# Fourteen expert-weight loads cut into 28 halves, one in each attention slot from 2 to 29

## The chip, the core and the metric

The kernel runs on one core of a Trainium2 chip. The metric is the device time of one execution in microseconds (us), the median of several runs. One more execution was taken with the hardware profiler; all rows below are from that one.

The engines of the core, as the profile names them: PE does matrix products and transposes through the array (PEld is its weight load), DVE and ACT do elementwise work, POOL does small copies and here also issues one kind of DMA, and SP only issues DMAs. DMAs issued by POOL run as queue q0 (software descriptors), those issued by SP as queue q1; both share 16 DMA engines.

## The reference: what is computed

Block-causal attention over 8 batches, 8 heads, 576 positions and 64 columns a head, followed by a mixture of experts on the 512 columns of the heads together. In short:

```python
scores = (q @ k.T) / sqrt(64)            # masked by blocks of 64
x = softmax(scores) @ v                  # (8, 576, 512)
logits = x @ w_gate                      # 8 experts
e = argmax(logits), or the expert of the position before where
    sigmoid(x @ w_local) >= 0.5          # a chain along each batch
out = p[e] * (relu(x @ w1[e]) @ w2[e])   # w1: 512x1024, w2: 1024x512
```

There are 4608 rows and 8 experts; each row goes through one expert alone.

## The kernel before: slots of attention, then tiles of rows

**Attention** runs as 32 slots, `i = 0 .. 31`, one for each pair of heads of a batch. A slot does the products with `v` of the pair before (`values`, line 998), its own scores (line 977) and exponentials, and the transposes of `k` and `q` of the pair after (`transposes(i + 1)`, tile `kq`, line 692). Its inputs come in stages: SP issues the loads of `k` and `q` of pair `i + 2` at the slot's start (`load_qk`, lines 867 and 872) and of `v` of pair `i + 1` (line 889); near the slot's end POOL copies `k` and `q` of pair `i + 2` into the order that the transposes want (`arrange`, line 880). PE reads the arranged copy in the slot after.

**Beside attention** two more things go through POOL's instruction stream. The finished rows `x` and their factors are stored to a table in DRAM (`x_rows`, line 677): the stores are held back during a slot and issued by POOL at its end (`release`). And the experts' weights are loaded with a cast from f32 to bf16: `load_weights(e, layer)` issues one DMA for all of `w1[e]` (line 107, 128 partitions x 4 rows of 1024) or of `w2[e]` (line 111, 128 x 8 rows of 512), 1 MB each as it lands. Fourteen of them, experts 0 to 6, go out in the even slots 2 to 28:

```python
if wload < 2 * E - 2 and i == 2 + 2 * wload:
    load_weights(*divmod(wload, 2))
    wload += 1
```

The last expert's two loads are placed apart, since its space is scratch and staging until then: `w1[7]` among the first gathers in slot 29 (the list `pending`), `w2[7]` at the end of slot 30. The staging of even pairs lies in the space of `w2[6]`.

**The experts** follow. The rows, sorted by expert, are gathered in tiles of 128 (`gather`, line 651, POOL), transposed by a DMA that SP issues (line 1269 for the first four tiles, 1393 after), multiplied by `w1` (`first_mm`, line 1093) and by `w2` (`second_mm`, line 1335). Which expert a tile belongs to is known only at run time, so the slice of `w2_bf` that `second_mm` reads is dynamic, and its first product waits for the loads of all eight `w2`. PE does the work in a fixed order: `first_mm` of tile 0, `first_mm` of tile 1, `second_mm` of tile 0, and so on.

What sets the order: every engine's stream is fixed when the kernel is built, in the order in which the Python code emits it. A POOL DMA carries one of eight completion semaphores in rotation (`order` of a POOL stream shows them as waits), so each waits for the one eight before it. The last part of the routing (the chain of lines 313 to 397 and `slots_first`, lines 430 to 537) is interleaved with the slots on DVE and PE.

Of the kernel before, what the change touches and what calls it, by code (L numbers as in the profile page):

```python
# [62 lines left out]
def kernel(  # L63
# [11 lines left out]
    nc = tc.nc  # L75
# [10 lines left out]
    Dm = H * D  # L86
    E = moe_w_gate.shape[1]
    F = moe_w1.shape[2]
    BS = B * S
    P = 128  # L90
# [11 lines left out]
    w1_bf = w_p.tile([P, E * KO1 * F], BF16, tag="w1", name="w1_bf")  # L102
    w2_bf = w_p.tile([P, E * FO * Dm], BF16, tag="w2", name="w2_bf")
    WE = KO1 * F
    def load_weights(e, layer):
        if layer == 0:
            nc.gpsimd.dma_start(
                out=w1_bf[:, e * WE:(e + 1) * WE].rearrange("p (do f) -> p do f", f=F),
                in_=moe_w1[e].rearrange("(do di) f -> di do f", di=P))
        else:  # L110
            nc.gpsimd.dma_start(
                out=w2_bf[:, e * WE:(e + 1) * WE].rearrange("p (fo d) -> p fo d", d=Dm),
                in_=moe_w2[e].rearrange("(fo fi) d -> fi fo d", fi=P))

    HP = H // 2
    NPAIR = B * HP
# [715 lines left out]
    with tc.tile_pool(name="atn_const", bufs=1) as cst, \  # L832
# [24 lines left out]
        def load_qk(i):  # L857
            if i >= NPAIR:
                return
            b, p = divmod(i, HP)  # L860
            h2 = slice(2 * p, 2 * p + 2)
            tl = ld.tile([P, 2, D], F32, tag="qkl", name="qkl")
            raws[i] = [tl]
            for j, src in enumerate((k, q)):

                m = staged_of(i)[:, j].rearrange("p (h j d) -> p h j d", h=2, j=4)
                nc.sync.dma_start(
                    out=m.rearrange("p h j d -> p h (j d)"),
                    in_=src[b, h2, :512].rearrange("h (p j) d -> p h (j d)", j=4))
                raws[i].append(m)  # L870
            for j, src in enumerate((k, q)):
                nc.sync.dma_start(out=tl[64 * j:64 * j + 64],
                                  in_=src[b, h2, 512:].rearrange("h s d -> s h d"))
# [34 lines left out]
        half = []  # L908
# [19 lines left out]
        def transposes(i, ahead=0, between=lambda: None):  # L928
            if i >= NPAIR:
                return between()  # L930
            ps = psp.tile([P, 2, 512], F32, tag="sc", name="kq")


            for j in range(9):
                if j == ahead:
                    turn_tail(i)()
                    between()
                if j < 8:
                    turn_part(i, j // 4, ps, (j % 4,))
            to = qkTs[i % 2][:, :, :512]  # L940
            if i == 1:
                for copy, part in zip(copies, range(2)):
                    copy(to[:, part].rearrange("p (r s) -> p r s", r=2),
                         ps[:, :, QA * part:QA * part + QA])
            else:
                nc.scalar.copy(to.rearrange("p a (r s) -> p r a s", r=2),
                               ps.rearrange("p r (a s) -> p r a s", a=2))
# [34 lines left out]
        def exps(i, u, ps):  # L982
            if i >= NPAIR:
                return
            for col, n, c, q0 in EXPS[u]:
                rows = slice(0, P)
                nc.scalar.activation(exps_at(i, c, q0, n, rows), ps[rows, :, col:col + n],  # L987
                                     func=AF.Exp, scale=scale_attn)
# [88 lines left out]
        def weights_at(w, ev):  # L1077
            nc.vector.tensor_copy(w, w1_bf[:, bass.ds(ev, WE)])
            return w
# [21 lines left out]
        def expert(ph, j, engines=(mybir.EngineType.PE, mybir.EngineType.DVE)):  # L1101
            return nc.values_load(
                et_i[ph][0:1, j:j + 1], engines=engines, min_val=0,
                max_val=(E - 1) * WE,
                skip_runtime_bounds_check_because="the table is clamped to the last expert")

        def bf(x, n):
            return x.rearrange("p a s -> p (a s)").bitcast(BF16)[:, :n]
# [33 lines left out]
        wload = 0  # L1142
# [28 lines left out]
        def behind(i):  # L1171

            def between():
                if i % HP == 2 and i < NPAIR - 2 or i == NPAIR - HP or not routing(i) and i > 1:
                    vector(AHEAD_OF[i % HP])
                run(sums)
                if sums:
                    routing(i)

            sums = sums_of(i)  # L1180
            if sums:
                values(i - 1, between)
            else:
                values(i - 1)
                between()
            if not swap:
                add_chunks(i - 1)
            if i == NPAIR - 2:
                mask(i - 1, nc.vector)
            load_v(i + 1)  # L1190
            if i > 1 and not rows_first(i):
                vector(AFTER[i % HP])

        def rows_first(i):
            return i % HP == 3 and NPAIR // 2 < i < NPAIR - 1

        holding[0] = True
        for i in range(NPAIR):
            slot[0] = i
            load_qk(i + 2)  # L1200


            swap = i == 1
            if not swap:
                behind(i)
            if i == NPAIR - 1:

                tiles = [(0, j) for j in range(NS[0])] + [(1, j) for j in range(NS[1])]
                ev = {j: expert(*tiles[j]) for j in range(2)}
                w = weights_at(bf(Pc[0], WE), ev[0])  # L1210
            for u in range(len(UNITS)):
                ps = scores(i, u)
                if u < 2 or i < 2:
                    exps(i, u, ps)
                if u == 0:
                    if i == 0:
                        transposes(1, 8)
                        constants()
                        for h in range(2):
                            hs = slice(64 * h, 64 * h + 64)  # L1220
                            nc.sync.dma_start(
                                out=wg2[hs, :, 16 * h:16 * h + E],
                                in_=moe_w_gate.rearrange("(p h d) e -> h d p e", h=2, d=D)[h])
                            nc.sync.dma_start(
                                out=wg2[hs, :, 16 * h + E:16 * h + E + 1],
                                in_=moe_w_local.rearrange("(p h d) e -> h d p e", h=2, d=D)[h])
            if swap:
                behind(i)
            last = lambda: exps(i, 2, ps) if i > 1 else None
            if i == NPAIR - 2:  # L1230
                last()
                last = lambda: None
                run([lambda: half_batch(B - 1, 0)])
            if i:
                transposes(i + 1, 6 if swap else 0,
                           last)
            if swap:
                add_chunks(i - 1)
            if i == NPAIR - 1:
                routing(i)  # L1240
            run(turns_of(i))
            if rows_first(i):
                vector(AFTER[i % HP])
            slot[0] = i + 0.5
            if i % HP == 0 or NPAIR - 3 <= i < NPAIR - 1:
                routing(i)
            if i < NPAIR - 1:
                vector(END[i % HP])
            early_mask = i % 2 == 0 and i <= NPAIR // 2
            if early_mask:  # L1250
                mask(i - 1, nc.gpsimd)
            arrange(i + 2, [nc.gpsimd.tensor_copy] * 2)
            if not early_mask and i != NPAIR - 2:
                mask(i - 1, nc.gpsimd)
            while pending:
                pending.pop(0)()

            if wload < 2 * E - 2 and i == 2 + 2 * wload:
                load_weights(*divmod(wload, 2))
                wload += 1  # L1260
            if i < NPAIR - 1:
                release(queue=nc.gpsimd)
            if i == NPAIR - 2:

                free = bf(Sb[(NPAIR - 3) % NSB], 2 * S * 2)[:, -AHEAD * Dm:]
                xTs = {}
                for j in range(AHEAD):
                    xTs[j] = free[:, j * Dm:(j + 1) * Dm].rearrange("p (k n) -> p k n", k=KO1)
                    nc.sync.dma_start(out=xTs[j], in_=row_of_x(xgs[j]), transpose=True)
                load_weights(E - 1, 1)  # L1270
# [20 lines left out]
    with ExitStack() as ffn:  # L1291
# [143 lines left out]
        for i, (ph, j) in enumerate(tiles):  # L1435
            now, done = w, prev
            waiting = len(held)
            if i == 0:
                w = w_next
            elif i + 1 < len(tiles):  # L1440
                w = w_third if i == 1 else weights_of(i + 1)
# [28 lines left out]
            if i == behind_tile:  # L1470

                nc.gpsimd.drain()
                n = nc.values_load(used[0:1, 0:1], min_val=0, max_val=E * BS)
                with tc.If(n > NS[1] - MORE, label="more"):  # L1474
                    more_tiles()
        i = len(tiles) - 1
# [37 lines left out]
```

## Time and profile before

| | |
|---|---|
| median of 3 runs | 411.5 us (409.78 to 412.72) |
| the profiled execution | 408.54 us |
| its span, first to last instruction | 406.5 us |
| PE busy | 392.6 us (97%) |
| DVE, ACT, POOL busy | 60%, 56%, 48% |
| mean granted TensorE clock | 1.000 |
| HBM read, written | 66.88 MB, 14.70 MB |
| weight loads on q0 | 16 of 1024 KB, 9.9 us median from issue to landing |

The slots run from about 7 us to 257 us after the span's start, the experts from there to the end. An engine is busy while it works on an instruction; issuing a DMA is not counted as busy. In a list of waits a row names the engine and tile that waited, what ended the wait, and its total, count and longest.

### The profile page before, as it was taken

The page shows a single profiled execution, that of the slowest core. Times are in us where ns is not written, and L with a number is a line of the kernel's source. Part 1 is how long each engine was busy: PE and PEld are TensorE (multiplying, and loading weights), DVE is VectorE, ACT ScalarE, POOL GpSimd, SP SyncE. Part 2 cuts the span into 40 slices and gives each one's busy share as a digit, 9 for nine tenths or more (in the row PEclk, how much of TensorE's full clock was granted, in tenths as well). Part 3 has the DMA queues.
Part 4 walks back from the last instruction along what each step waited for, and adds up shares of the span by engine and source line. Part 5 has one row for each costly group of instructions (what it writes and reads, how often), then busy time and mean ns, then how long its engine had stood idle before and what let it go on. Part 6 is the DMA issues. An engine that isn't in the chain of part 4 may idle for free. (4 is left out here: it accounts for less than half of the span.)

```text
span 406.5 us, 14547 instructions
## 1 busy us (share of the span) xinstructions
PE 392.6 (97%) x5834; PEld 285.5 (70%) x5834; DVE 242.2 (60%) x505; ACT 228.7 (56%) x391; POOL 196.1 (48%) x250
## 2 busy tenths in 40 slices
PE   9999999999999999999998998998999999999985
PEld 7667677677677677667766666666777777777763
DVE  2463564564564577967899975977887333333320
ACT  3758557567557557657647465333545555555542
POOL 1244251342341342582632363074776888888833
PEclk9999999999999999999999999999999999999999
DMA  6588989999999979999989689944763645655532
GB/s 178 142 190 194 216 172 222 201 201 228 194 202 210 183 183 246 174 202 244 170 192 237 136 155 192 151 109 120 166 168 97 170 135 148 154 149 149 128 99 78
DMA packets 108819, 69.97 MB, mean 172 GB/s; under 512 B 74847, under 2 KB 100255, under 8 KB 108752
## 3 DMA queue, kind: packets, MB, share of 16 engines
q0 software_dynamic: 19200, 34.84, 41.6%
q1 hardware_dynamic: 89552, 34.19, 37.2%
q8 instruction: 48, 0.79, 0.8%
q14 instruction: 19, 0.16, 0.1%
HBM read 66.88 MB, written 14.70 MB: 201 GB/s over the span
## 5 line engine op out<-in xcount | busy, mean ns | idle before, releaser
L1019 DVE TENSOR_TENSOR S<-S,Pc 128x896 f32<-128x896 f32 (+2 forms) x96 | 84.0, 875 | 23.9 <-PE o L998 19.1
L977 PE MATMUL sc<-qkT 64*64 64x224 f32 (+6 forms) x1536 | 91.6, 367 | 0.0
L1297 DVE COPY w1c<-w_bf 128x4096 bf16 x36 | 44.3, 1231 | 55.6 <-PE ps_h L1093 52.8
L1093 PEld LDWEIGHTS <-w1c 128*128 128x128 bf16 x1152 | 67.2, 98 | 9.1 <-issue 1.3
L880 POOL COPY w_bf<-w_bf 128x512 f32<-128x512 f32 x61 | 43.9, 737 | 60.8 <-DMA w_bf<-in_k_dram 33.0
L977 PEld LDWEIGHTS sc<-qkT 64*64 64x64 f32 x1536 | 70.5, 134 | 3.7 <-issue 2.5
L1335 PE MATMUL ps_y<-w_bf,hT 128*128 x296 | 69.9, 379 | 1.0 <-DMA w_bf<-in_moe_w_dram 1.0
L987 ACT ACTIVATE Pc<-sc 128x448 f32<-128x448 f32 (+1 forms) x96 | 68.1, 716 | 0.0
L1093 PE MATMUL ps_h<-xT,w1c 128*128 128x128 bf16 x1088 | 66.3, 219 | 1.3 <-ACTq L1474 1.1
L1343 POOL DMA_INDIRECT out_dram<-y,idx x37 | 56.2, 1519 | 22.0 <-ACT y L1340 12.2
L651 POOL DMA_INDIRECT xg<-x_rows,idx x38 | 47.1, 1239 | 31.3 <-issue 13.9
L1096 ACT ACTIVATE hT<-ps_h 128x512 bf16<-128x512 f32 x76 | 45.3, 597 | 26.2 <-PE ps_h L1093 24.6
L998 PE MATMUL o<-Pc,v 128*64 128x320 f32 (+2 forms) x512 | 57.3, 366 | 0.0
L998 PEld LDWEIGHTS o<-Pc,v 128*64 128x64 f32 x512 | 34.6, 137 | 24.1
L1340 ACT ACTIVATE y<-ps_y,xg 128x512 f32<-128x512 f32 x37 | 25.4, 687 | 45.5 <-PE ps_y L1335 39.1
L987 ACT ACTIVATE S<-sc 128x576 f32<-128x576 f32 x64 | 42.0, 656 | 12.6 <-PE sc L977 12.1
L1335 PEld LDWEIGHTS <-hT 128*128 128x128 bf16 x296 | 27.5, 98 | 27.3 <-issue 1.0
L1011 ACT COPY oT<-o 128x576 f32<-128x576 f32 x32 | 20.5, 641 | 35.7 <-PE o L1007 35.7
L1026 POOL MEMSET S<- 64x128 f32 x30 | 6.0, 200 | 69.8 <-DVE S L1021 40.7
L818 DVE TENSOR_TENSOR xg<-trx,rs 128x512 bf16<-128x512 f32 (+1 forms) x31 | 20.2, 685 | 25.9 <-PE trx L692 25.8
L998 PE MATMUL o<-S,v 128*64 128x192 f32 (+1 forms) x256 | 34.7, 392 | 0.3 <-ACT qkT L925 0.3
L714 ACT COPY LT<-trg 128x320 f32<-128x320 f32 x15 | 6.4, 426 | 44.4 <-PE trg L705 44.4
(313 smaller groups left out, 467.4 us busy)
## 6 DMA issues: line engine op xcount, KB each, us to landing
w_bf<-in_moe_w_dram POOLq DMA_DIRECT2D x16, 1024.0 KB, 9.9
w_bf<-in_k_dram SPq DMA_DIRECT2D x32, 256.0 KB, 3.4
w_bf<-in_q_dram SPq DMA_DIRECT2D x32, 256.0 KB, 7.7
v<-in_v_dram SPq DMA_DIRECT2D x64, 128.0 KB, 5.8
x_rows<-xg POOLq DMA_DIRECT2D x24, 128.0 KB, 8.1
qkl<-in_k_dram SPq DMA_DIRECT2D x32, 32.0 KB, 3.8
qkl<-in_q_dram SPq DMA_DIRECT2D x32, 32.0 KB, 5.7
vl<-in_v_dram SPq DMA_DIRECT2D x32, 32.0 KB, 7.4
```

Source lines behind the costliest of these rows:

```text
L651: st = nc.gpsimd.indirect_dma_start(out=x, out_offset=None, in_=x_dram[:rows], in_offset=bass.IndirectOffsetOnAxis(ap=row_of(ph, j), axis= ...
L880: copies[j](m, raws[i][1 + j].rearrange("p h j d -> p j h d"))
L977: nc.tensor.matmul(to[:, col + skip:col + n], lhsT=t[r, 0, k0:k0 + ST], rhs=t[r, 1, q0 + skip:q0 + n], start=True, stop=True)
L987: nc.scalar.activation(exps_at(i, c, q0, n, rows), ps[rows, :, col:col + n], func=AF.Exp, scale=scale_attn)
L998: nc.tensor.matmul(po[64 * h:64 * h + 64, VO + q0:VO + q0 + n], lhsT=vs[i][c][:, h, :], rhs=exps_at(i, c, q0, n, slice(0, P))[:, h, :], st ...
L1019: nc.vector.tensor_add(Ss[i][:, :, P * c:], Ss[i][:, :, P * c:], Pc[i % 2][:, :, POS[c]:POS[c] + n])
L1093: nc.tensor.matmul(ps[:, fo, :], lhsT=w[:, ko * F + f0:ko * F + f0 + P], rhs=xT[:, ko, :], start=(ko == 0), stop=(ko == KO1 - 1))
L1096: relu[0] = nc.scalar.activation(hT[:, half * (FO // 2):(half + 1) * (FO // 2), :], ps, func=AF.Relu)
L1297: ended["w"] = nc.vector.tensor_copy(w, w1_bf[:, bass.ds(ev[i], WE)])
L1335: nc.tensor.matmul(ps, lhsT=hT[:, fo, :], rhs=w2_bf[:, bass.ds(ev + fo * Dm, Dm)], start=(fo == 0), stop=(fo == FO - 1))
L1340: nc.scalar.activation(y, ps, func=AF.Copy, scale=factor)
L1343: st = nc.gpsimd.indirect_dma_start(out=out_flat, out_offset=bass.IndirectOffsetOnAxis(ap=row_of(ph, j), axis=0), in_=y, in_offset=None, b ...
```

## The change

`load_weights` takes a third argument, `half`. With it the load covers half of the rows of each partition: two of the four rows of `w1[e]`, four of the eight of `w2[e]`, half a MB as it lands. The slots issue 28 such halves, one in each of the slots 2 to 29, in the same order as before. The two loads of expert 7 stay whole and where they were.

```diff
-    def load_weights(e, layer):
-        if layer == 0:
-            nc.gpsimd.dma_start(
-                out=w1_bf[:, e * WE:(e + 1) * WE].rearrange("p (do f) -> p do f", f=F),
-                in_=moe_w1[e].rearrange("(do di) f -> di do f", di=P))
-        else:
-            nc.gpsimd.dma_start(
-                out=w2_bf[:, e * WE:(e + 1) * WE].rearrange("p (fo d) -> p fo d", d=Dm),
-                in_=moe_w2[e].rearrange("(fo fi) d -> fi fo d", fi=P))
+    def load_weights(e, layer, half=None):
+        w, x, n = ((w1_bf, moe_w1, F), (w2_bf, moe_w2, Dm))[layer]
+        r = slice(0, WE // n) if half is None else slice(half * WE // n // 2, (half + 1) * WE // n // 2)
+        nc.gpsimd.dma_start(
+            out=w[:, e * WE:(e + 1) * WE].rearrange("p (o n) -> p o n", n=n)[:, r],
+            in_=x[e].rearrange("(o i) n -> i o n", i=P)[:, r])
...
-            if wload < 2 * E - 2 and i == 2 + 2 * wload:
-                load_weights(*divmod(wload, 2))
+            if wload < 4 * E - 4 and i == 2 + wload:
+                load_weights(*divmod(wload // 2, 2), wload % 2)
                 wload += 1
```

DVE's stream is the same instruction for instruction; PE, ACT and SP differ in buffer numbers alone. Lines below the change move up by three (line 677 becomes 674, 880 becomes 877, 1335 becomes 1332), and all weight loads have line 108.

POOL's stream at the end of attention, slots 28 to 30, before (`w_bf<-w_bf` is the arranging copy, `S` a mask, `xg<-x_rows` a gather, `x_rows<-` a store of rows; 128x8x512 is a whole `w2`, 128x4x1024 a whole `w1`):

```order
L1026 MEMSET S 64x2x64
L111 DMA w_bf<-in_moe_w_dram 128x8x512
L677 DMA x_rows<-xg 64x256
L880 COPY w_bf<-w_bf 128x512 x2
L1026 MEMSET S 64x2x64
L651 DMA xg<-x_rows,idx_89 128x257 x2
L107 DMA w_bf<-in_moe_w_dram 128x4x1024
L651 DMA xg<-x_rows,idx_89 128x257 x2
L677 DMA x_rows<-x 128x256 x2
L677 DMA x_rows<-xg 64x256
L111 DMA w_bf<-in_moe_w_dram 128x8x512
```

The same place after the change:

```order
L1023 MEMSET S 64x2x64
L108 DMA w_bf<-in_moe_w_dram 128x4x512
L674 DMA x_rows<-xg 64x256
L877 COPY w_bf<-w_bf 128x512 x2
L1023 MEMSET S 64x2x64
L648 DMA xg<-x_rows,idx_89 128x257 x2
L108 DMA w_bf<-in_moe_w_dram 128x4x1024
L648 DMA xg<-x_rows,idx_89 128x257 x2
L108 DMA w_bf<-in_moe_w_dram 128x4x512
L674 DMA x_rows<-x 128x256 x2
L674 DMA x_rows<-xg 64x256
L108 DMA w_bf<-in_moe_w_dram 128x8x512
```

The load of `w2[6]` in slot 28 has become a half, and its second half stands in slot 29, behind the four gathers and `w1[7]`, ahead of the row stores and of `w2[7]`.

POOL's stream in slots 20 and 21, before, up to the first two of the eight stores of factors (the others follow in the same alternation):

```order
L1026 MEMSET S 64x2x64
L111 DMA w_bf<-in_moe_w_dram 128x8x512
L677 DMA x_rows<-xg 64x256
L880 COPY w_bf<-w_bf 128x512 x2
L1026 MEMSET S 64x2x64
L677 DMA x_rows<-factors 128x4x1
L677 DMA x_rows<-factors 64x1
```

The same place after:

```order
L1023 MEMSET S 64x2x64
L108 DMA w_bf<-in_moe_w_dram 128x4x512
L674 DMA x_rows<-xg 64x256
L877 COPY w_bf<-w_bf 128x512 x2
L1023 MEMSET S 64x2x64
L108 DMA w_bf<-in_moe_w_dram 128x4x512
L674 DMA x_rows<-factors 128x4x1
L674 DMA x_rows<-factors 64x1
```

A half now stands directly ahead of the eight stores of factors, so that the eighth of them takes the half's completion semaphore.

## The prediction

> **What bounds the kernel now.** First the page's busy times, then a table by stage. Columns after the stretch: its length, and busy time (and count) of PE, PEld, DVE, ACT and POOL, the granted clock, the DMA share, GB/s.
>
> ```profile
> PE 392.6 (97%) x5834; PEld 285.5 (70%) x5834; DVE 242.2 (60%) x505; ACT 228.7 (56%) x391; POOL 196.1 (48%) x250
> 20.00:60.00 40.00, 40.00 (x682) 28.71 (x682) 22.82 (x39) 24.90 (x44) 17.12 (x40) 1.00 0.90 193
> ...
> 180.00:220.00 40.00, 40.00 (x692) 28.70 (x690) 33.57 (x94) 24.59 (x44) 16.26 (x27) 1.00 1.00 201
> 220.00:240.00 20.00, 17.51 (x315) 12.84 (x317) 17.90 (x42) 10.47 (x18) 6.09 (x11) 1.00 0.83 176
> 240.00:257.00 17.00, 15.68 (x250) 10.54 (x241) 11.39 (x25) 8.38 (x15) 7.47 (x9) 1.00 1.09 177
> 257.00:290.00 33.00, 30.00 (x358) 21.96 (x354) 26.99 (x83) 14.14 (x24) 15.62 (x13) 1.00 0.59 130
> 290.00:406.00 116.00, 110.78 (x1260) 80.69 (x1256) 47.81 (x64) 58.13 (x94) 83.69 (x60) 1.00 0.52 136
> ```
>
> From 20 to 220 us, where 26 of the 28 halves go, PE has no gap, though the DMA engines are at 0.90 to 1.00. The experts are PE's too. So weight loads cost time only where PE waits for one. The list of PE's waits, filtered to PE, names one such place:
>
> ```profile
> PE sc L975 <- DVE xg L818: 1.8, 1, 1.8
> PE ps_y L1335 <- DMA w_bf<-in_moe_w_dram: 1.0, 1, 1.0
> ```
>
> The timeline around it (start, length, engine, line, work, idle before it and its releaser):
>
> ```profile
> 244.25 1.01 POOL L651 DMA_INDIRECT xg<-x_rows,idx  x1 [0.31 <-issue]
> 246.66 1.16 POOL L677 DMA_DIRECT2D x_rows<-x  x2 [1.40 <-DVE x L818]
> 248.38 0.93 POOL L111 DMA_DIRECT2D w_bf<-in_moe_w_dram  x1
> 259.75 1.96 PE L1093 MATMUL ps_h<-S,qkT 128*128 128x128 bf16 x32
> 262.69 1.89 PE L1335 MATMUL ps_y<-w_bf,hT 128*128 x8 [0.97 <-DMA w_bf<-in_moe_w_dram]
> 265.93 0.49 DVE L710 TENSOR_TENSOR LTl<-LTl,trg 128x320 f32<-128x320 f32 x1 [0.91 <-PE trg L705]
> ```
>
> `w2[7]` is issued at 248.38; PE ends tile 1's `first_mm` at 259.75 + 1.96 = 261.71 and stands 0.97 us until it has landed. That is 14 us after its issue, against the page's 9.9 median for such loads. The DMA queues by window show why. The rows of 244:261 come first, then 246:248, 260:261, 261:262 and 262:263; each gives packets, MB, and the time as a share of 16 engines:
>
> ```profile
> q0 software_dynamic: 1761, 2.65, 99.0%
> ...
> q0 software_dynamic: 198, 0.41, 109.9%
> ...
> q1 hardware_dynamic: 412, 0.10, 76.2%
> q0 software_dynamic: 119, 0.11, 66.0%
> ...
> q1 hardware_dynamic: 266, 0.10, 111.5%
> q0 software_dynamic: 15, 0.01, 6.3%
> ...
> q1 hardware_dynamic: 264, 0.22, 76.4%
> q0 software_dynamic: 1, 0.00, 0.1%
> ```
>
> From 244 to 261 us q0 is full (99.0%) and its last packet falls just before PE goes on. `w2[7]` lands late because everything issued ahead of it on q0 is served first, and PE is already waiting for the end of that queue: whatever is put into it there is paid one for one.
>
> **The change part by part.** *The half in slot 29.* The second half of `w2[6]` now follows the fourth gather (244.25 + 1.01) and precedes the row stores, which wait for DVE until 246.66; the issue fits into that 1.40 us of idle time, so `w2[7]` is still issued near 248.4. But 0.5 MB (0.524 million bytes as it lands, which is how the rows count) is now ahead of it. In slot 28, where it was before, q0 had time: the row of 238:240, before the gathers begin in earnest, reads
>
> ```profile
> q0 software_dynamic: 20, 0.02, 5.0%
> ```
>
> so nothing is won by its having left. Its price is its service time. At the mean rate of the full stretch, 2.65 MB in 17 us = 0.156 MB/us, it is 3.4 us. The best row, 0.41 MB in 2 us with nothing on q1, gives 2.6 us; the worst with q1 busy, 0.11 MB in 1 us, gives 4.8. Between: before, q1 moved 0.10 + 0.22 MB from 261 to 263, when q0 was all but empty. Now the two share that time; at 0.11 for q0 and 0.10 for q1, q1's 0.32 MB lasts 3.2 us, in which q0 moves 0.35; the remaining 0.17 at 0.156 takes 1.1; together 4.3 us. I take **4.0 us**, nearer to the shared reading, bounds 2.6 and 4.8.
>
> The gathers and `w1[7]` stand ahead of the half and are not delayed; the transposes of the first tiles run on q1 beside a q0 that was full already. Behind the wait all moves with PE: DVE's next step on routing, L710, waits for PE's `trg` itself (0.91 us), so DVE gains no lead, and the experts' stages are PE's to the end (110.78 of 116.00). No later stall absorbs the 4.0.
>
> *The other 27 halves.* POOL issues 28 DMAs for 14. The rows of one issue (count, then ns min/median/max) for a whole `w1`, a whole `w2` and a store of 128 KB or less:
>
> ```profile
> L107 POOL DMA_DIRECT2D w_bf<-in_moe_w_dram x8: 754/802/971, 24.7 to 241.8; - x8
> L111 POOL DMA_DIRECT2D w_bf<-in_moe_w_dram x8: 905/905/954, 40.4 to 248.4; - x8
> L677 POOL DMA_DIRECT2D x_rows<-xg x31: 540/542/570, 55.9 to 247.8; - x31
> ```
>
> A half lies between 0.54 and 0.9; at an estimated 0.65, POOL issues 28 x 0.65 - 14 x 0.85 = 6 us more over 28 slots. POOL is busy for 48% of the span. What waits behind it is the arranging copy for PE's transposes, and the tightest new place is slot 21, where the eighth store of factors now shares the semaphore of the half issued 5 us before:
>
> ```profile
> 171.35 5.28 POOL L677 DMA_DIRECT2D x_rows<-factors  x8 [0.52 <-DVE rs L794]
> 176.67 1.48 POOL L880 COPY w_bf<-w_bf 128x512 f32<-128x512 f32 x2
> 185.37 0.67 PE L692 MATMUL kq<-id_f,w_bf 64*128 64x64 f32 x16
> ```
>
> The copies end at 178.15, PE reads them at 185.37: 7.2 us of cover. The half needs 2.6 to 4.8 us of service from 171; a wait of 0 to 3 us on POOL is hidden. Cost 0; if the cover were gone, the excess over 7.2.
>
> The Trainium skill's page "DMA: Bandwidth & Descriptors" (section "Rules for kernel authors") wants at least 1 MiB per DMA, and "Anatomy of one DMA" gives about 2.0 us fixed plus bytes over 436 GB/s, which would make the half 3.2 us. The trace has q0 at 99.0% with DMAs behind one another, where a fixed share is not to be seen; the sum goes by the rows.
>
> *Less crowding in the even slots.* POOL's waits for `k` and `q` shrink, which no PE wait from 20 to 220 us would repay. Gain 0; bound of a gain in the rivals.
>
> **Sum.** Span 406.5 + 4.0 = 410.5; with the 408.54 - 406.5 = 2.04 us around it, 412.5 against 408.54. The median of the runs is 411.5, so on it **415.5 us**, +1.0%.
>
> **The rivals.** *A, the wait cools TensorE.* PE would stand 0.97 + 4.0 = 5 us, longer than anywhere in this trace (1.8). At the span's start the same 16 transposes of `k` and `q` took
>
> ```profile
> 8.70 1.12 PE L692 MATMUL kq<-id_f,w_bf 64*128 64x64 f32 x16
> 24.66 0.67 PE L692 MATMUL kq<-id_f,w_bf 64*128 64x64 f32 x16
> ```
>
> a factor of 1.67, some 9 us after PE's first work. Should the wait bring that back for 9 us, 9 x (1 - 0.67/1.12) = 3.6 us more are lost: 415.5 + 3.6 = 419.1; for half as long, 417.3. Against it: the clock row reads 1.00 at the start as well, and no pause of this length is in the trace. The Trainium skill's page "TensorE: Matmul & The Clock Gate" (Part 1) has the array fall to half rate after an idle window of about 3.4 us and recover after as much work; by its free-running window a 5 us pause may or may not hold a whole one. Chance 0.22.
>
> *B, the tail hides it.* If what PE waits for at 262.4 is not q0's end but a slowest engine's receipt, or if the half slips into gaps that a share of 99.0% hides, `w2[7]` lands within 1 us of now: 411.5 to 412.5. Against it, the sum of MB in the stretch. Chance 0.13.
>
> *C, faster.* Plain runs take 411.5 - 408.54 = 3.0 us more than the profiled one. Should that be `k` and `q` arriving late beside whole weight loads, the halves would give it back: 408.5 if the half in slot 29 cost nothing, 412.5 with it. It decides if the attention slots of plain runs hold DMA waits that this trace, with PE at 40.00 of 40.00, does not have. A gain over 1% needs yet more than the 3.0. Chance 0.08.
>
> *D, POOL's semaphores.* The wait in slot 21 exceeds 7.2 us, by 1 to 3: 416.5 to 418.5 together with the tail. Chance 0.05.
>
> **How the numbers follow.** The forecast has 0.52, with 414.1 to 416.3 as its own range. One per cent is 4.1 us (407.4 and 415.6), about what measurement of this kernel tells from no change; the forecast lies at that line, so it gives 0.28 to "same" and 0.24 to "slower". A and D are slower (0.27), B the same (0.13), C half faster, half the same (0.04 each): faster 0.04, same 0.45, slower 0.51. The range runs from 411.0, which leaves out the better part of C and the edge of B, to 419.0, which leaves out the longer half of A.
>
> **What would show it.** In the changed kernel's profile: PE's wait at `ps_y` (then line 1332) of 3.6 to 5.8 us against 0.97; q0 full until about 265 to 266; 40.00 of 40.00 for PE up to 220 us; L1090 and L1332 at today's durations after the wait (A would show them longer for some us). A wait of 1 us at `ps_y` makes the forecast wrong; so does a PE wait on a copy of line 877.

## The result, and the profile after

The changed kernel takes 414.37 us (median of 22 runs, 411.63 to 419.23), the kernel before 411.81 (22 runs, 408.59 to 418.68): 1.0080 times the time before, 95% interval 1.0059 to 1.0101, or +3.3 us (2.4 to 4.2). Forecast were +4.0 us and a ratio of 1.0097. Ratios here and below leave disturbed runs out, so that they are not exactly the quotients of the medians. The profiled execution took 411.63 us with a span of 409.8, against 408.54 and 406.5.

The page's busy times of the changed kernel, and its table by stage, to hold against the same stretches of before:

```profile
PE 391.7 (96%) x5834; PEld 284.1 (69%) x5834; DVE 244.0 (60%) x505; ACT 227.1 (55%) x391; POOL 198.8 (49%) x264
```

```profile
20.00:60.00 40.00, 40.00 (x698) 29.47 (x702) 21.44 (x38) 26.31 (x47) 17.95 (x45) 1.00 0.95 203
...
180.00:220.00 40.00, 39.85 (x699) 29.09 (x703) 33.78 (x93) 24.80 (x45) 21.45 (x33) 1.00 1.08 205
...
257.00:290.00 33.00, 27.38 (x306) 19.38 (x307) 26.29 (x81) 12.02 (x21) 15.51 (x12) 1.00 0.60 123
```

PE works as long as before and is spread over a longer span. Two stretches lost: 257 to 290 us has 27.38 us of PE's work in place of 30.00, and the attention slots, which had no gap from 20 to 220 us, now have one (39.85 of 40.00 here, 39.61 in 140 to 180). PE's waits name the places:

```profile
PE ps_y L1332 <- issue: 2.3, 1, 2.3
PE ps_h L1090 <- DVE w1c L1294: 1.7, 1, 1.7
...
PE ps_h L1090 <- DVE x L815: 1.2, 1, 1.2
...
PE trg L702 <- POOL S L1023: 0.5, 1, 0.5
```

**The end of attention.** Traces are lined up below at a mark in the slots: the row `o<-id_f,qkl`, the first of the slot's transposes for the next pair, called the slot's first product here and in the expectations. It stands late in the slot's code, so that the stretch from one such row to the next, called the slot's length, holds the values, sums and scores that the code has in the slot after. The timeline, with slot 30's first product in its first row:

```profile
243.09 0.28 PE L689 MATMUL o<-id_f,qkl 64*128 64x64 f32 x2
...
243.99 0.82 POOL L108 DMA_DIRECT2D w_bf<-in_moe_w_dram  x1
...
245.73 1.14 POOL L674 DMA_DIRECT2D x_rows<-x  x2 [0.92 <-DVE x L815]
...
247.45 0.93 POOL L108 DMA_DIRECT2D w_bf<-in_moe_w_dram  x1
...
256.79 1.29 DVE L815 TENSOR_TENSOR x<-trx,rs 128x512 bf16<-128x512 f32 x2 [1.14 <-DMA x_rows<-x]
...
258.14 1.07 PE L1090 MATMUL ps_h<-S,Pc 128*128 128x128 bf16 x16 [1.16 <-DVE x L815]
...
259.91 1.95 PE L1090 MATMUL ps_h<-S,qkT 128*128 128x128 bf16 x32
...
264.11 1.89 PE L1332 MATMUL ps_y<-w_bf,hT 128*128 x8 [2.26 <-issue]
```

PE now stands twice. The half is issued at 243.99. The row stores at 245.73 are behind it on q0, and they read the tile `x`; DVE's last writes of `x` (L815) wait 1.14 us until those stores have landed, and PE's second part of tile 0 waits 1.16 us for DVE. (In the kernel `ps_h` and the transposes that L815 reads take turns in three buffers for PE's results, tag `sc`, which would explain that wait.) Then comes the wait at the first `ps_y`: 2.26 us against 0.97. (The trace finds no releaser for it and says "issue"; in experiments 3, 5 and 10 the same wait is put down to the weights' DMA.) From slot 30's first product to `ps_y` it is 264.11 - 243.09 = 21.02 us, before

```profile
244.35 0.28 PE L692 MATMUL o<-id_f,qkl 64*128 64x64 f32 x2
```

262.69 - 244.35 = 18.34: **2.7 us more**. q0 in 244:261 and in 263:264 of the changed kernel:

```profile
q0 software_dynamic: 2052, 2.87, 95.3%
...
q0 software_dynamic: 16, 0.01, 5.8%
```

In windows of 0.2 us its last packets fall in 263.2 to 263.4, and in 262.0 to 262.2 before: counted from slot 30, 2.5 us later.

**Slot 22.** The timeline of PE and POOL there, before and then after:

```profile
176.39 0.28 PE L692 MATMUL o<-id_f,qkl 64*128 64x64 f32 x2
...
178.21 0.20 POOL L1026 MEMSET S<- 64x128 f32 x1
...
181.01 1.26 PE L705 MATMUL trg<-S,sel 128*32 128x320 f32 x16
...
185.26 0.28 PE L692 MATMUL o<-id_f,qkl 64*128 64x64 f32 x2
```

```profile
174.29 0.28 PE L689 MATMUL o<-id_f,qkl 64*128 64x64 f32 x2
...
177.95 0.55 POOL L674 DMA_DIRECT2D x_rows<-factors  x1 [3.51 <-DMA w_bf<-in_moe_w_dram]
...
179.90 0.20 POOL L1023 MEMSET S<- 64x128 f32 x1
...
180.15 1.27 PE L702 MATMUL trg<-S,sel 128*32 128x320 f32 x12 [0.55 <-POOL S L1023]
...
184.42 0.28 PE L689 MATMUL o<-id_f,qkl 64*128 64x64 f32 x2
```

The eighth store of factors waits 3.51 us for the half's semaphore. Behind it on POOL stands not only the arranging copy but also the clearing of `S`, which PE's sums `trg` read next. Before, `S` was clear at 178.41 and read at 181.01: 2.6 us of cover. Counted from the slot's first product, `S` is now clear 5.81 us in (180.10 - 174.29) against 2.02 (178.41 - 176.39), 3.79 us later; less the cover, 1.2 us are PE's. (PE's row shows only 0.55 us of it as a wait; the sums as a whole end 7.13 us after the slot's first product, before 5.88.) The slot is 184.42 - 174.29 = 10.13 us long against 8.87.

**The rest of the 3.1 us between the two profiled executions** can't be put down to the change. Slot 1's first product starts at 16.62 us, before at 18.31, which gains 1.7. The twelve traces of this study fall into two groups there, 16.5 to 17.2 us (six) and 18.2 to 18.3 (six). The change has no part in it, since the first weight load is issued only later, at 25.12 us (24.72 before). PE's first products run slowly for some time, and in before for longer, as the same four products show, before and then after:

```profile
5.62 1.22 PE L1114 MATMUL idle<-const-float32-0.0 128*128 128x128 f32 x4
...
5.46 0.71 PE L1111 MATMUL idle<-const-float32-0.0 128*128 128x128 f32 x4
```

The granted clock's row reads 1.00 there in both. In the experts' stretch, from the first `ps_y` to the span's end, 1.9 us more go (145.7 against 143.8), in short stops that come at other places in every trace; the nine traces in which PE did no work there at a granted clock below 1.00 have 143.8 (before and experiment 9) to 149.0 us (experiment 8) for this same work. So two single traces compare well stage by stage, and badly end to end.

### The profile page after: what moved, and what is told of

It reads as the page before. It is cut to its first block, busy times and chain, and to the rows that moved or that the text cites. A ratio compares the mean times of both kernels' runs of the same rounds, so it can differ in the third digit from the quotient of the medians.

```text
span 409.8 us, 14566 instructions
## 1 busy us (share of the span) xinstructions
PE 391.7 (96%) x5834; PEld 284.1 (69%) x5834; DVE 244.0 (60%) x505; ACT 227.1 (55%) x391; POOL 198.8 (49%) x264
## 4 chain that ended last, share of the span: by engine, by line
PE 67%; DVE 9%; issue 9%; POOL 6%; DMA 6%; ACT 1%; POOLq 1%; DVEq 0%; SPq 0%; ACTq 0%
PE sc L974 15%; PE o L995 15%; PE ps_h L1090 11%; PE ps_y L1332 10%; PE trg L702 5%; PE kq L689 3%; DMA x_rows<-x 3%; DVE S L1016 3%; DMA out_dram<-y,idx 2%; POOL out_dram L1340 2%; POOL xg L648 2%; PE o L1004 2%; PE trx L689 2%; PE o L689 1%; POOL x_rows L674 1%
## 5 line engine op out<-in xcount | busy, mean ns | idle before, releaser
L1016 DVE TENSOR_TENSOR S<-S,Pc 128x896 f32<-128x896 f32 (+2 forms) x96 | 85.2, 888 | 21.4 <-PE o L995 16.5
L974 PE MATMUL sc<-qkT 64*64 64x224 f32 (+6 forms) x1536 | 90.4, 364 | 0.0
L1294 DVE COPY w1c<-w_bf 128x4096 bf16 x36 | 45.4, 1261 | 55.7 <-PE ps_h L1090 33.2
L877 POOL COPY w_bf<-w_bf 128x512 f32<-128x512 f32 x61 | 46.6, 777 | 60.2 <-DMA w_bf<-in_k_dram 21.3
L648 POOL DMA_INDIRECT xg<-x_rows,idx x38 | 49.3, 1298 | 42.6 <-issue 16.9
L1340 POOL DMA_INDIRECT out_dram<-y,idx x37 | 44.9, 1214 | 23.5 <-issue 9.5
L1008 ACT COPY oT<-o 128x576 f32<-128x576 f32 x32 | 20.5, 640 | 35.7 <-PE o L1004 35.7
L815 DVE TENSOR_TENSOR xg<-trx,rs 128x512 bf16<-128x512 f32 (+1 forms) x31 | 20.2, 685 | 26.3 <-PE trx L689 26.1
```

Of the source, the lines that this page charges most:

```text
L648: st = nc.gpsimd.indirect_dma_start(out=x, out_offset=None, in_=x_dram[:rows], in_offset=bass.IndirectOffsetOnAxis(ap=row_of(ph, j), axis= ...
L877: copies[j](m, raws[i][1 + j].rearrange("p h j d -> p j h d"))
L974: nc.tensor.matmul(to[:, col + skip:col + n], lhsT=t[r, 0, k0:k0 + ST], rhs=t[r, 1, q0 + skip:q0 + n], start=True, stop=True)
L1016: nc.vector.tensor_add(Ss[i][:, :, P * c:], Ss[i][:, :, P * c:], Pc[i % 2][:, :, POS[c]:POS[c] + n])
L1294: ended["w"] = nc.vector.tensor_copy(w, w1_bf[:, bass.ds(ev[i], WE)])
L1340: st = nc.gpsimd.indirect_dma_start(out=out_flat, out_offset=bass.IndirectOffsetOnAxis(ap=row_of(ph, j), axis=0), in_=y, in_offset=None, b ...
```

## The experiments

Four theories. T, the prediction's: what costs is the half MB that stands in q0 ahead of the last row stores and of `w2[7]`. P: POOL's wait in slot 21 reaches PE through `S`. N: 28 DMAs cost more than 14. A, the rival: a pause cools TensorE. Experiments 1 to 4, 5 to 8, and 9 and 10 ran together, each group against runs of before of its own. "Lateness" below is the time from slot 30's first product to the first `ps_y`; before it is 18.34 us, after 21.02.

### 1. The halves, but `w2[6]` whole in slot 28

```diff
-            if wload < 4 * E - 4 and i == 2 + wload:
+            if wload < 4 * E - 6 and i == 2 + wload:
                 load_weights(*divmod(wload // 2, 2), wload % 2)
                 wload += 1
+            elif i == 28:
+                load_weights(E - 2, 1)
```

> Halves in the slots 2 to 27 as in the change, but w2[6] goes out whole in slot 28, as before; nothing is loaded in slot 29 but w1[7]. Theory T (the half in slot 29 is paid at the end of q0): most of the 3.3 us go, the time is 411.5 to 412.8 us against 411.8, PE's wait at ps_y is about 1 us again and DVE's wait for the stores of x is gone. Theory P (the eighth store of factors in slot 21 waits for the half's completion, the mask that PE's sums read comes late): 1.3 us of the change's cost stay, about 413.1, with the POOL wait of 3.5 us still in the trace. Theory N (28 DMAs cost more than 14 wherever they stand): the time stays at 415.

Measured: 1.0038 (0.9996 to 1.0081). The trace has neither wait at the end; the eighth store of factors and the first `ps_y` read, in its timeline:

```profile
177.25 0.55 POOL L674 DMA_DIRECT2D x_rows<-factors  x1 [2.58 <-DMA w_bf<-in_moe_w_dram]
...
259.97 1.89 PE L1334 MATMUL ps_y<-w_bf,hT 128*128 x8
```

Lateness 259.97 - 242.45 = 17.52 us. With 26 halves and their DMAs still there, the loss at the tail is gone from the trace. The runs alone would not show it: +1.6 us, with an interval (-0.2 to 3.3) that reaches the change's own loss. POOL waits 2.58 us here, about the cover, and slot 22 is only 9.07 us long (174.52 to 183.59). Far from both places, among the experts, this trace has a pause of 2.14 us with A behind it:

```profile
389.59 3.53 PE L1090 MATMUL ps_h<-xT,w1c 128*128 128x128 bf16 x32 [2.14 <-ACTq L1473]
```

The pause began at 387.45; the granted clock falls to 0.50 at about 389.5 and is back at 1.00 by 393, and the 32 products take 3.53 us in place of 1.95.

### 2. The same, and slot 21's half in slot 20

```diff
-            if wload < 4 * E - 4 and i == 2 + wload:
-                load_weights(*divmod(wload // 2, 2), wload % 2)
-                wload += 1
+            if wload < 4 * E - 6 and i == 2 + wload and i != 21:
+                for _ in range(1 + (i == 20)):
+                    load_weights(*divmod(wload // 2, 2), wload % 2)
+                    wload += 1
+            elif i == 28:
+                load_weights(E - 2, 1)
```

> As the run with w2[6] whole in slot 28, and besides the half of slot 21 goes out with that of slot 20, so that no half stands right ahead of the eight stores of factors. T and P together: the time of before, 411.8 +- 0.8; POOL's wait of 3.5 us at the eighth store and PE's wait for the mask are gone. T alone: no difference from the run before it. N: 415.

Measured: 0.9991 (0.9951 to 1.0032). Slot 22 is 8.87 us long (176.09 to 184.96), as before. Twenty-six halves cost nothing that the runs can tell once these two places are mended, which refutes N, and win nothing.

### 3. Whole loads, and only `w2[6]` in two halves, in slots 28 and 29

```diff
-            if wload < 2 * E - 2 and i == 2 + 2 * wload:
+            if wload < 2 * E - 3 and i == 2 + 2 * wload:
                 load_weights(*divmod(wload, 2))
                 wload += 1
+            elif i in (28, 29):
+                load_weights(E - 2, 1, i - 28)
```

> The loads of before, whole and in even slots, except that w2[6] alone is cut, one half in slot 28 and one in slot 29. T: slower by 2 to 4 us than before, 413.8 to 415.8, with the waits of the change at the end of attention (DVE for the stores of x, PE at ps_y 2 us or more). P: 2 us, since slot 21 is as before. N: the time of before.

Measured: 1.0121 (1.0063 to 1.0178). This one half is enough for the whole of the change's loss; by the runs it costs 5.0 us (2.6 to 7.3), above the 2 to 4 expected. Lateness 264.76 - 244.08 = 20.68 us, and behind the wait something that the change's own trace does not have. The timeline first, then the windows from 265 us on (the granted clock is the third number from the end of a row):

```profile
264.76 2.86 PE L1334 MATMUL ps_y<-w_bf,hT 128*128 x8 [2.28 <-DMA w_bf<-in_moe_w_dram]
267.55 1.95 PE L702 MATMUL trg<-S,sel 128*32 128x320 f32 x16
```

```profile
265.00:266.00 1.00, 1.00 (x5) 0.43 (x4) 0.86 (x5) 0.00 (x0) 0.00 (x0) 0.77 0.00 0
266.00:267.00 1.00, 1.00 (x4) 0.30 (x2) 0.34 (x2) 0.00 (x0) 0.32 (x1) 0.50 0.02 8
...
269.00:270.00 1.00, 1.00 (x19) 0.57 (x11) 0.36 (x1) 0.00 (x0) 0.69 (x2) 1.00 0.36 70
```

The granted clock falls to 0.50 at about 265.5, 3.0 us after the pause began (262.48), with PE already at work again, and is back at 1.00 by 269. The same eight products take 2.86 us in place of 1.89 and the sums 1.95 in place of 1.28: 1.6 us on top. That is rival A, after a pause of 2.28 us.

### 4. Whole loads, and half of `w2[7]` ahead of the gathers

```diff
+            if i == 29:
+                load_weights(E - 1, 1, 0)
             while pending:
                 pending.pop(0)()
...
-                load_weights(E - 1, 1)
+                load_weights(E - 1, 1, 1)
```

> The loads of before, but w2[7] is cut: its first half goes out in slot 29 ahead of the first gather, where q0 is nearly idle, its second half stays at the end of slot 30. T: half a MB less stands at the end of q0; PE's wait of 0.97 us at ps_y goes, and the time falls by 0.5 to 1.5 us, 410.3 to 411.3; the first gathers land up to 3 us later without a PE wait. If the end of q0 isn't what PE waits for, no difference. If the gathers are late for the first tile, slower by 1 to 2 us.

Measured: 1.0000 (0.9960 to 1.0041). The `ps_y` wait is gone, as expected, but DVE waits 0.51 us for the row stores, PE stops twice for 0.2 to 0.3 us, and lateness is about 18.2 us (260.65 - 242.49). The gain of 0.5 to 1.5 us that was expected is not seen, in this trace or in the runs, whose interval would have room for it.

### 5 and 6. The dose: half of `w2[6]`, or all of it, read once more in slot 29 of the kernel before

```diff
             if wload < 2 * E - 2 and i == 2 + 2 * wload:
                 load_weights(*divmod(wload, 2))
                 wload += 1
+            if i == 29:
+                load_weights(E - 2, 1, 1)
```

`load_weights` is the change's; in experiment 6 the added call is `load_weights(E - 2, 1)`.

> The kernel before with its whole loads, and the second half of w2[6] read once more in slot 29 (0.5 MB, written over itself with the same numbers), ahead of slot 29's row stores. Queue theory T: what counts is the half MB that stands in q0 ahead of the last row stores and of w2[7], not how the other loads are cut. So the tail is that of the changed kernel: a wait of 0.5 to 1.5 us of TensorE for the arranged x tile (which waits for the landing of earlier row stores), a wait of 1.8 to 3 us at the first ps_y, ps_y 2.0 to 2.5 us later than before when both traces are lined up at slot 30, no wait at the mask in slot 22; 1.005 to 1.008 of the time before. Cooling theory A: the pause of TensorE is then about as long as in the run that split w2[6] alone, 2.3 us, so some executions show a granted clock of about 0.5 for 3 us after it and lose 1.7 us more; 1.008 to 1.012. If the split itself were the cost (a transfer in two pieces is slower than in one), this kernel, which splits nothing that anyone waits for, would stay at 1.000.

> The same with all of w2[6] read once more in slot 29 (1 MB). Queue theory T: twice the dose, so q0's last packets and the first ps_y come 4.0 to 4.6 us later than before when lined up at slot 30, of which the wait for the x tile takes more than before (2.5 to 3.5 us) and the wait at ps_y 1.5 to 3 us; 1.010 to 1.013 of the time before. Cooling theory A: the pauses sum to over 4 us, the granted clock falls to 0.5 for about 3 us behind them in the profiled execution, the first ps_y takes 2.9 us in place of 1.9 and the sums behind it 1.9 in place of 1.3, so 1.5 to 2 us come on top: 1.014 to 1.019. If the tail absorbed such delays (rival B), this kernel would not differ from the one with half the dose.

Measured: 1.0082 (1.0045 to 1.0120) for the half, 1.0187 (1.0107 to 1.0266) for the whole. The half, which no one needs, gives the change's tail: 0.96 us for `x`, 2.48 us at `ps_y`, lateness 265.51 - 244.48 = 21.03 us (2.7 more than before, just above the 2.0 to 2.5 expected), with the clock at 1.00. The whole, by its timeline and by its windows from 262 us on:

```profile
261.70 0.69 DVE L815 TENSOR_TENSOR x<-trx,rs 128x512 bf16<-128x512 f32 x1 [5.13 <-DMA x_rows<-x]
...
264.09 1.89 PE L1090 MATMUL ps_h<-S,Pc 128*128 128x128 bf16 x16 [6.12 <-DVE x L815]
...
269.86 1.89 PE L1334 MATMUL ps_y<-w_bf,hT 128*128 x7
```

```profile
262.00:264.00 2.00, 0.00 (x0) 0.00 (x0) 1.05 (x3) 0.00 (x0) 0.00 (x0) 0.52 1.32 110
264.00:266.00 2.00, 1.91 (x20) 1.71 (x24) 2.00 (x5) 0.00 (x0) 0.00 (x0) 0.50 1.21 195
```

Here the whole wait is for the row stores, against the expectation of two: PE stands 6.12 us for `x`, and when it comes to `ps_y` the weights are there. Lateness 269.86 - 244.14 = 25.72 us, 7.4 more than before; of these 2.2 are the cold clock's (the 16 products 1.89 in place of 1.07 us, the sums 1.30 for 0.75, the next 32 products 2.78 for 1.95). Twice the bytes cost 5.2 us without the clock, against 2.7 for once, each by one trace: about T's proportion, though above the 4.0 to 4.6 us expected, and A on top of it.

### 7. The change, with the half behind the row stores

```diff
-            if wload < 4 * E - 4 and i == 2 + wload:
+            if wload < 4 * E - 4 and i == 2 + wload and i < 29:
                 load_weights(*divmod(wload // 2, 2), wload % 2)
                 wload += 1
...
             if i == NPAIR - 2:
+                load_weights(E - 2, 1, 1)
```

> The changed kernel, with the second half of w2[6] put behind the row stores that follow it, directly ahead of w2[7]. T: the bytes ahead of w2[7] are the same, those ahead of the row stores are half a MB less. So DVE's wait for the row stores of x and TensorE's wait behind it (1.16 us in the changed kernel) go, the wait at the first ps_y grows by as much (2.3 to between 3.2 and 3.8 us), ps_y starts at the same place when lined up at slot 30, within 0.4 us, and the time is that of the changed kernel: 1.006 to 1.011 of the time before. If the two waits were separate losses that add up, the time would fall by about 1.1 us, to 1.004 to 1.006. Cooling A: one pause of 3.2 us or more in place of two short ones, so the granted clock falls to 0.5 behind it in the profiled execution, and 1.5 to 2 us come on top: 1.011 to 1.015.

Measured: 1.0160 (1.0112 to 1.0208), twice the change's loss. Its timeline, and its windows from 264 us on:

```profile
259.25 1.96 PE L1090 MATMUL ps_h<-S,qkT 128*128 128x128 bf16 x32
...
265.85 0.59 PE L1333 MATMUL ps_y<-w_bf,hT 128*128 x1 [4.64 <-issue]
```

```profile
264.00:266.00 2.00, 0.15 (x1) 0.21 (x2) 0.75 (x4) 0.00 (x0) 0.00 (x0) 0.60 0.19 48
266.00:268.00 2.00, 1.78 (x5) 0.65 (x5) 0.00 (x0) 0.00 (x0) 0.61 (x1) 0.50 0.00 0
268.00:270.00 2.00, 2.00 (x12) 0.55 (x14) 0.00 (x0) 0.54 (x1) 1.50 (x2) 0.50 0.28 66
```

The wait for `x` is gone, as expected, and `ps_y` comes no earlier for it, which bears out that the two waits are one queue seen twice. But the remaining one is 4.64 us and not 3.2 to 3.8, lateness 265.85 - 243.46 = 22.39 and not 21.0. The bulk of q0 is through at about 263.8, 20.3 us after slot 30's first product, as in the change (263.2, 20.1); behind it a trickle of two to four packets in each 0.2 us goes on until 265.2, and why is open. And one pause of 4.64 us cools the clock: 0.50 until about 271 us, `ps_y` and `trg` together 2.6 us longer than in the change.

### 8. Whole loads, and only `w2[4]` in two halves, in slots 20 and 21

```diff
-            if wload < 2 * E - 2 and i == 2 + 2 * wload:
+            if wload == 9 and i in (20, 21):
+                load_weights(*divmod(wload, 2), i - 20)
+                wload += i - 20
+            elif wload < 2 * E - 2 and i == 2 + 2 * wload:
                 load_weights(*divmod(wload, 2))
                 wload += 1
```

> The kernel before with one load alone cut in two: w2[4], its halves in slots 20 and 21. Semaphore theory P: the eighth store of the factors in slot 21 waits for the half that was issued eight DMAs before it, GpSimd stands 2.5 to 3.5 us, its mask comes late, and TensorE waits 0.5 to 1.5 us for the mask at the sums of slot 22: the stretch from slot 22's first product to slot 23's is 9.2 to 10.2 us long in place of 8.87, and slots from 23 to the end run 0.3 to 1.3 us late; time 1.001 to 1.003 of before, below what the runs can tell. If the stall in the changed kernel came from how much is queued at that time and not from which DMA the store waits for, slot 22 keeps its 8.87 us and GpSimd's wait at the factors stays under 1.2 us.

Measured: 1.0011 (0.9969 to 1.0052), too coarse to tell P from nothing, as expected; the timeline does.

```profile
176.75 0.28 PE L689 MATMUL o<-id_f,qkl 64*128 64x64 f32 x2
...
180.59 0.55 POOL L674 DMA_DIRECT2D x_rows<-factors  x1 [3.46 <-DMA w_bf<-in_moe_w_dram]
...
182.79 1.27 PE L702 MATMUL trg<-S,sel 128*32 128x320 f32 x12 [0.72 <-POOL S L1023]
...
187.05 0.28 PE L689 MATMUL o<-id_f,qkl 64*128 64x64 f32 x2
```

That one half in slot 21 is enough for the wait of 3.46 us, and slot 22 is 187.05 - 176.75 = 10.30 us long, 1.4 more than before and just above the expected range. P holds for the place. Of its size, the four traces with a half in slot 21 give 1.3 (the change), 1.4 and, with POOL's wait at 2.58 and 2.63, 0.2 and 0.3 us (experiments 1 and 7). This goes with how late `S` is clear after the slot's first product: 5.81, 5.98, 4.75 and 4.85 us, where the sums that read it come at about 4.6.

### 9. Whole loads, `w2[6]` one slot earlier

```diff
-            if wload < 2 * E - 2 and i == 2 + 2 * wload:
+            if wload < 2 * E - 2 and i == 2 + 2 * wload - (wload == 13):
```

> The kernel before, with its whole loads, but the load of w2[6] one slot earlier, in slot 27. Queue theory T, with the sign turned: about a MB less stands in q0 ahead of the last row stores and of w2[7], so q0's last packets come 3 us or more earlier than before when lined up at slot 31's first product, TensorE has no wait at the first ps_y and none for the x tile, and ps_y starts up to 1.0 us earlier than before, no more, since before's wait there is 0.97 us: 0.997 to 0.999 of the time before, less than the runs can tell. If before's wait at ps_y were set by something else than the queue, the wait would stay at about 1 us in the trace. Dose line: with minus 1 MB the ps_y start lies 0 to 1 us earlier, with plus 0.5 MB 2.7 us later, with plus 1 MB 5 us later and more with a cold clock: flat on one side, steep on the other.

(The product meant is slot 30's, in this expectation and the next.) Measured: 1.0015 (0.9971 to 1.0059), and the timeline goes against the expectation:

```profile
264.35 1.89 PE L1332 MATMUL ps_y<-w_bf,hT 128*128 x7 [1.88 <-DMA w_bf<-in_moe_w_dram]
```

The wait is 1.88 us, not none, and lateness 264.35 - 243.84 = 20.51 us. The premise was wrong: issued in slot 28 (at 228.13 in before), `w2[6]` had left q0 before the gathers began, as the prediction's own row of 238:240 showed, so an earlier issue could take nothing out of the queue. From 245 to 265 us q0 moves 2.55 MB before and 2.45 here. That lateness was still 2.2 us above before's is counted here to the spread of this tail for the same bytes, below; its cause is open.

### 10. The change, with slot 21's half in slot 20

```diff
-            if wload < 4 * E - 4 and i == 2 + wload:
-                load_weights(*divmod(wload // 2, 2), wload % 2)
-                wload += 1
+            if wload < 4 * E - 4 and i == 2 + wload and i != 21:
+                for _ in range(1 + (i == 20)):
+                    load_weights(*divmod(wload // 2, 2), wload % 2)
+                    wload += 1
```

> The changed kernel, but slot 21's half goes out in slot 20 beside the one that is there: the half in slot 29 stays. T and P together: the stretch from slot 22's first product to slot 23's is 8.87 us as before and no wait for the mask is seen in slots 22 and 23, while the tail is the change's: TensorE waits 0.8 to 1.2 us for the x tile and 2.2 to 2.6 us at the first ps_y, which starts 2.3 to 2.8 us later than before when lined up at slot 31; 1.005 to 1.008 of the time before, against 1.008 for the change with its mask stall. If the mask's stall weighed nothing in the end, 1.008 to 1.010. Cooling A: if the granted clock falls to 0.5 after the pause at ps_y in the profiled execution, another 1.6 us are lost there; with pauses of this length it has fallen in one of three traces so far.

Measured: 1.0042 (1.0004 to 1.0079); slot 22 back at 8.87 us (175.36 to 184.23), and the tail that of the change, with a longer wait for `x` than expected, by the timeline:

```profile
258.75 1.07 PE L1090 MATMUL ps_h<-S,Pc 128*128 128x128 bf16 x16 [2.01 <-DVE x L815]
...
264.92 1.89 PE L1333 MATMUL ps_y<-w_bf,hT 128*128 x7 [2.47 <-DMA w_bf<-in_moe_w_dram]
```

Lateness 264.92 - 243.47 = 21.45 us, 3.1 more than before (2.3 to 2.8 expected), and no cooling after 2.47 us.

### The traces together

| what stands in q0 at the end | lateness of the first `ps_y`, us | clock at 0.50 behind the wait |
|---|---|---|
| as before (before, 1, 8, 2, 9) | 18.34, 17.52, 18.12, 19.68, 20.51; mean 18.8 | in none |
| a half more (3, after, 5, 10) | 20.68, 21.02, 21.03, 21.45; mean 21.0 | in one of four |
| a half more, behind the stores (7) | 22.39 | yes |
| a whole load more (6) | 25.72 | yes |

The half costs 2.2 us by the means, 2.7 by the pair of before and after. With the same bytes queued the tail still varies by 3 us from trace to trace, so that a single pair of traces could pass this off as an effect; but the four with a half more all lie above the five without. By the runs, the kernels with the tail's half alone (3, 5, 10) have 1.0121, 1.0082 and 1.0042, those with slot 21's and not the tail's (1, 8) 1.0038 and 1.0011; the means, +3.4 and +1.0 us, add up to 4.4, which their own errors don't set apart from the change's 3.3 (2.4 to 4.2). No version here beats the kernel before: the best, experiment 2, is equal to it.

## Why the prediction was right, and where it was not

**The place and the mechanism: right.** The loss is at the end of attention, q0 is full there, and what is put into it is paid for. Experiment 3 shows that this one half suffices, experiment 1 that the tail's waits go with it, experiments 5 and 6 that bytes in the queue do it whatever they are. Rival B (the tail hides it) is out.

**The term of 4.0 us: too large.** Of its two readings, the shared one (4.3) was taken as the nearer. The pair of traces gives 2.7 us, the means 2.2; the lower bound, 2.6 at q0's best rate, was the nearest. The bulk of q0's packets did move by about 3.2 us, counted from slot 30 (from about 261.3 to 263.2 on the clocks of two traces that differ by 1.26 there), near the 3.4 of the mean rate. But before, PE went on not with the bulk but behind a trickle of eight packets that ended 1 us after it, in 262.0 to 262.2, which is part of the 0.97 us; so less than the bulk's delay reached PE. q0 was through at 263.4, which is 264.7 on the clock of before, and not at 265 to 266.

**"PE's wait at `ps_y` of 3.6 to 5.8 us": wrong.** It is 2.26 us. The prediction had the row stores in its order listing, behind the half, and asked only when they would be issued, not who waits for them to land. DVE does, since `x` has two buffers, and PE for DVE: 1.16 us of the same delay are paid there, before `ps_y`. The two make 3.4 us, against 0.97 + 2.7 = 3.7; experiment 7 bears out that they are one.

**"The other 27 halves: cost 0": wrong by about 1 us.** The prediction found the semaphore in slot 21 and bounded POOL's wait by 0 to 3 us (3.51 came), but measured the cover on the arranging copy, 7.2 us. The next instruction on POOL behind that copy, the clearing of `S`, has 2.6. It was queued behind the same wait and its reader is PE. Experiments 8, 1 and 7 bear out both the place and that only the excess over the cover counts. With it, "40.00 of 40.00 up to 220" fell too (39.61 in 140:180, 39.85 in 180:220). Neither of the prediction's two signs of being wrong came, a wait of 1 us at `ps_y` or a PE wait on a copy of line 877; the wait that came behind POOL was for another tile. That the DMAs' number costs nothing was right (experiment 2).

So a term too large by 1.3 to 1.8 us and a missing one of about 1 nearly cancel, and 415.5 against 414.37 is better than its steps: that much is luck.

**Rival A, 0.22: it happens.** Not in the change's profiled execution, but in one of four traces with this tail, at 1.6 us, and in both with a longer pause, at 2.2 and 2.6; the estimates were 1.8 to 3.6. The reading "the clock row reads 1.00 at the start as well" said nothing about pauses: behind these the row falls to 0.50 plainly, and what the slow start with its 1.00 is stays open.

How often the changed kernel's plain runs have it can't be read from their times, but each run's mean granted clock is on record, and bounds it. Over the runs behind the ratios it is 0.9956 in the changed kernel and 0.9971 to 0.9978 in the three groups of runs of before. The difference, 0.0015 to 0.0022 of 412 us, is 0.6 to 0.9 us by estimate, of the 3.3. Not even that is the tail's for certain: experiments 1 and 2, without its waits, have 0.9948 and 0.9962, and the mean takes in the clock's fall behind PE's last product, where nothing is lost (the change's own trace, at 0.997, has no other). Experiments 6 and 7, with 0.9910 and 0.9920, come to 2.5 and 2.1 us by the same estimate, near their traces' 2.2 and 2.6. The Trainium skill's page "TensorE: Matmul & The Clock Gate" (Part 1) has half rate after an idle window of about 3.4 us, with a free-running window. The 0.50 agrees, and so do the falls after 4.64 and 6.12 us. The shorter pauses do not: 2.14 us (experiment 1) and 2.28 us sufficed, where 2.01, 2.13, 2.26, 2.47, 2.48 and 2.57 us in five other traces did not, and what was measured here decides.

**Rival C (faster):** experiments 1 and 2 carry the 26 other halves and are not faster; the 3.0 us that it had in view would be 0.993, outside experiment 2's interval. **Rival D** asked for a wait above 7.2 us; the wait was smaller, and the cover too.

## What to carry to other kernels

Where a transfer is added to a queue that is full, list everything behind it on that queue, and for each the reader of its landing: buffers that a store must free count as much as data that a load must bring. Where an engine's instruction gets a new wait, take the cover of every instruction behind it on that engine, not of the next one; the smallest decides. And a delay that comes in two pauses can be cheaper than the same delay in one, since the clock fell behind two of eight pauses of 2.0 to 2.6 us here, and behind both longer ones.

## What was not expected of the hardware

The clock fell 2.1 to 4.1 us after a pause began (389.5 against 387.45 in experiment 1, 265.5 against 262.48 in 3, 264.4 against 261.21 in 7, 262.1 against 257.97 in 6), once after PE had resumed, and stayed at 0.50 for 3.4 to 6.8 us. The start of the span took one of two lengths, up to 1.7 us apart, before the first weight load was issued, with the clock's row at 1.00. And the tail with the same bytes in q0 took 17.5 to 20.5 us; what sets that is open.
